# Block-sparse attention and a gated MLP on one core: a list-scheduled order, row-halved scores, a 0/1 mask product and tokens dealt two to a partition

## The chip, the cores and the metric

The kernel runs on one core of a Trainium2 chip. The metric is the time of one execution on the device in microseconds (us). The profile's span, from the first to the last instruction, is about 2 us shorter than that time. Each profile shown here is of one execution. "PE" is TensorE's matmuls, "PEld" its weight loads, "DVE" VectorE, "ACT" ScalarE, "POOL" GpSimd, "SP" the queue that issues most DMAs.

## The reference, cut to what matters

```
q, k, v: (4 batches, 8 heads, 768 tokens, 64)      block = 32 tokens
scores = q @ k.T / 8
mask   = near the diagonal | first or last block row or column | 3 sampled blocks a row
attn   = softmax(where(mask, scores, -1e9))
x      = (attn @ v) as 3072 tokens x 512
h      = x @ w_in                      # 512 -> 2048
out    = (h * sigmoid(beta * h)) @ w_out   # 2048 -> 512
```

The MLP of a group of tokens needs the attention of all eight heads for these tokens. Attention is done for a pair of heads (there are four pairs in a batch) and a stretch of queries at a time.

## The kernel before: the parts that matter

A score matmul takes one head. It contracts over 88 rows: 64 of the head and 24 more, which hold a one-hot of the key's block on one side and the mask's penalty on the other, so the masked score comes out of TensorE ready.

```python
def step(hh, kc0):                         # one head, kn chunks of 128 keys
    def run():
        sc = sc_pool.tile([P, 1024], FP32, tag="sc", name="sc")
        for i in range(kn):
            nc.tensor.matmul(sc[:, i * n:(i + 1) * n],
                lhsT=kX[0:D + NB, hh, (kc0 + i) * P:(kc0 + i + 1) * P],
                rhs=qX[0:D + NB, hh, q0:q0 + n], start=True, stop=True)
        et = et_pool.tile([P, 1024], FP16, tag="et", name="et")
        nc.scalar.activation(out=et[:, 0:kn * n], in_=sc[:, 0:kn * n],
                             func=AF.Exp, bias=0.0, scale=SCALE)
...                                        # values: 24 matmuls of 65 columns, then normalise
tiles = [(0, 0, 512), (0, 512, 256), (1, 0, 256), (1, 256, 512), ...]
n_group = N_TOK // 512                     # six MLP groups of 512 tokens
```

The order is a hand-made weave: one MLP piece after so many score steps. Keys and queries are turned on TensorE for the first five pairs, by DMA after that; the attention results are always turned on TensorE. Six consecutive tokens lie in one partition, so a load comes in pieces of 1536 bytes.

The softmax here doesn't subtract the row's maximum and nothing guards it: scores larger than these inputs give would overflow.

Of the kernel before, what the change touches and what calls it, by code (L numbers as in the profile page):

```python
# [13 lines left out]
ALU = mybir.AluOpType  # L14


@with_exitstack
def kernel(
# [17 lines left out]
    NC = S // P  # L36
    NPAIR = H // 2
# [6 lines left out]
    NEG = -30000.0  # L44

    persist = ctx.enter_context(tc.tile_pool(name="persist", bufs=1))
    stage_pool = ctx.enter_context(tc.tile_pool(name="stage", bufs=3))
    et_pool = ctx.enter_context(tc.tile_pool(name="et", bufs=13))
    work_pool = ctx.enter_context(tc.tile_pool(name="work", bufs=3))
    g_pool = ctx.enter_context(tc.tile_pool(name="g", bufs=2))  # L50




    NVA = 5
    NSTG = 2
    va_tiles = []
    for i in range(NVA):
        va_tiles.append(persist.tile([P, 2, NC, VW], FP16, name=f"va_{i}"))
    stg = {}  # L60
    for nm in ("k", "q"):
        stg[nm] = [persist.tile([P, 2, NC, P], FP16, name=f"{nm}stg_{i}") for i in range(NSTG)]

    def pair_src(x, b, j):
        return x[b, 2 * j:2 * j + 2].rearrange("h (p c) d -> p h (c d)", c=NC)

    loaded = {}

    def emit_load(b, j, eng=None):
        eng = eng or nc.sync  # L70
        sts = []
        for name, src in (("k", k), ("q", q), ("v", v)):
            st32 = stage_pool.tile([P, 2, NC * D], FP32, tag=f"{name}st", name=f"{name}st")
            if (b, j) == (1, 0) and name == "k":
                nc.gpsimd.tensor_copy(out=st32[0:1, 0, 0:1], in_=w_out_sb[0:1, 4, 0:1])
            eng.dma_start(out=st32, in_=pair_src(src, b, j))
            sts.append(st32)
        loaded[(b, j)] = sts
# [3 lines left out]

# [4 lines left out]
    beta_h_sb = persist.tile([P, N_FFC], FP32, name="beta_h_sb")  # L87

# [3 lines left out]
    def gate(w, like):  # L92
        nc.gpsimd.tensor_copy(out=w[0:1, 0, 0:1], in_=like[0:1, 0, 0:1])

    def emit_w_in(i):
        nc.gpsimd.dma_start(out=w_in_sb[:, :, i * 512:(i + 1) * 512],
                            in_=w_in_r[:, :, i * 512:(i + 1) * 512])

    def emit_w_out(i):
        nc.gpsimd.dma_start(out=w_out_sb[:, i * 4:(i + 1) * 4, :],  # L100
                            in_=w_out_r[:, i * 4:(i + 1) * 4, :])


    sc_pool = ctx.enter_context(
        tc.tile_pool(name="sc_psum", bufs=2, space=bass.MemoryType.PSUM))
    av_pool = ctx.enter_context(
        tc.tile_pool(name="av_psum", bufs=1, space=bass.MemoryType.PSUM))
    mm_pool = ctx.enter_context(
        tc.tile_pool(name="mm_psum", bufs=3, space=bass.MemoryType.PSUM))

    NSET = 5
    sets = []
    for i in range(NSET):
        sets.append((persist.tile([P, 2, S], FP16, name=f"kX_{i}"),
                     persist.tile([P, 2, S], FP16, name=f"qX_{i}")))

    onehot = persist.tile([NB, NC, P], FP16, name="onehot")
    oh_flat = onehot.rearrange("j c p -> j (c p)")
    oh_tok = persist.tile([P, NC, NB], FP16, name="oh_tok")
    mask16 = persist.tile([NB, NB], FP16, name="mask16")  # L120
    warm = persist.tile([P, 512], FP16, name="warm")
    sc_warm = []

    def emit_warm(n):
        if not sc_warm:
            sc_warm.append(sc_pool.tile([P, 1024], FP32, tag="sc", name="warm_ps"))
        for _ in range(n):
            nc.tensor.matmul(sc_warm[0][:, 0:512], lhsT=warm[:, 0:P], rhs=warm,  # L128
                             start=True, stop=True)

    def emit_first():

        sb_i32 = persist.tile([NB, 3], mybir.dt.int32, name="sb_i32")
# [3 lines left out]
        nc.sync.dma_start(out=sb_i32, in_=sb_lo)  # L137
        nc.scalar.dma_start(out=beta_sb, in_=moe_beta.rearrange("(c p) -> c p", p=P))
        for j in range(3):
            emit_load(0, j)  # L140
# [3 lines left out]
        dif = persist.tile([NB, NB], FP32, name="dif")  # L144
        nc.gpsimd.iota(dif, pattern=[[1, NB]], base=0, channel_multiplier=-1,
                       allow_small_or_imprecise_dtypes=True)
        iota_j = persist.tile([NB, NB], FP32, name="iota_j")
        nc.gpsimd.iota(iota_j, pattern=[[1, NB]], base=0, channel_multiplier=0,
                       allow_small_or_imprecise_dtypes=True)
        iota_i = persist.tile([NB, 1], FP32, name="iota_i")  # L150
        nc.gpsimd.iota(iota_i, pattern=[[0, 1]], base=0, channel_multiplier=1,
                       allow_small_or_imprecise_dtypes=True)

        nc.gpsimd.memset(oh_tok, 1.0)
        nc.gpsimd.affine_select(out=oh_tok, in_=oh_tok, pattern=[[1, NC], [-BLK, NB]],
                                compare_op=ALU.is_ge, fill=0.0, base=0,
                                channel_multiplier=NC)
        nc.gpsimd.affine_select(out=oh_tok, in_=oh_tok, pattern=[[-1, NC], [BLK, NB]],
                                compare_op=ALU.is_ge, fill=0.0, base=BLK - 1,
                                channel_multiplier=-NC)  # L160
        make_identity(nc, identity)
        for va in va_tiles:
            nc.gpsimd.memset(va[:, :, :, D:VW], 1.0)
        nc.gpsimd.tensor_copy(out=ident32, in_=identity[0:16, 0:16])
        for i in range(NSTG):
            for nm in ("k", "q"):
                nc.gpsimd.memset(stg[nm][i][:, :, :, D + NB:P], 0.0)


        emit_warm(6)  # L170
        ohp = mm_pool.tile([P, NC, P], FP16, tag="mm", name="ohp")
        for c in range(NC):
            nc.tensor.transpose(out=ohp[0:NB, c, :], in_=oh_tok[:, c, :], identity=identity)  # L173
        nc.scalar.copy(out=oh_flat, in_=ohp[0:NB].rearrange("j c p -> j (c p)"))
        emit_warm(6)

        mask_blk = persist.tile([NB, NB], FP32, name="mask_blk")
# [9 lines left out]
        sb_f32 = persist.tile([NB, 3], FP32, name="sb_f32")  # L187
        nc.vector.tensor_copy(out=sb_f32, in_=sb_i32)
        for r in range(3):
            nc.vector.scalar_tensor_tensor(out=mask_blk, in0=iota_j,  # L190
                                           scalar=sb_f32[:, r:r + 1], in1=mask_blk,
                                           op0=ALU.is_equal, op1=ALU.max)
        nc.vector.tensor_scalar(out=mask16, in0=mask_blk, scalar1=1.0,
                                scalar2=-NEG, op0=ALU.subtract, op1=ALU.mult)
        for h in range(2):
            nc.scalar.copy(out=stg["k"][0][:, h, :, D:D + NB], in_=oh_tok)
        ps = mm_pool.tile([P, NC, NB], FP32, tag="mm", name="mkt")
        for c in range(NC):
            nc.tensor.matmul(ps[:, c, :], lhsT=oh_flat[:, c * P:(c + 1) * P],
                             rhs=mask16, start=True, stop=True)  # L200
        for h in range(2):
            nc.scalar.copy(out=stg["q"][0][:, h, :, D:D + NB], in_=ps)

    def emit_more_columns():
        for i in range(1, NSTG):
            for nm in ("k", "q"):
                for h in range(2):
                    nc.scalar.copy(out=stg[nm][i][:, h, :, D:D + NB],  # L208
                                   in_=stg[nm][0][:, h, :, D:D + NB])

    def emit_beta():
        ps = mm_pool.tile([P, 512], FP32, tag="mm", name="bet")
        nc.tensor.transpose(out=ps[:, 0:N_FFC], in_=beta_sb, identity=ident32)
        nc.vector.tensor_scalar(out=beta_h_sb, in0=ps[:, 0:N_FFC], scalar1=0.5,
                                scalar2=None, op0=ALU.mult)


    prepared = {}
    n_prep = [0]

    N_PE_PREP = 5

    def emit_cast(x):
        b, j = seq[x]
        kst, qst, vst = loaded.pop((b, j))
        kX, qX = sets[x % NSET]
        va = va_tiles[x % NVA]
        for name, st32, dst in (("k", kst, kX), ("q", qst, qX)):
            st16 = stg[name][x % NSTG]
            nc.vector.tensor_copy(out=st16[:, :, :, 0:D],  # L230
                                  in_=st32.rearrange("p h (c d) -> p h c d", d=D))
            if x >= N_PE_PREP:
                nc.sync.dma_start_transpose(
                    out=dst.rearrange("p h (c s) -> p (h c) s", s=P),
                    in_=st16.rearrange("p h c e -> p (h c e)"))
        prepared[(b, j)] = (kX, qX, va, vst)

    def emit_cast_v(x):
        _, _, va, vst = prepared[seq[x]]
        nc.vector.tensor_copy(out=va[:, :, :, 0:D],  # L240
                              in_=vst.rearrange("p h (c d) -> p h c d", d=D))
# [11 lines left out]

    def attn_steps(b, j, q0, n):

        nq = n // P
        kn = 2 if n == 512 else 3
        ets = [[None] * NC, [None] * NC]

# [247 lines left out]
```

## Time and profile before

| | before |
|---|---|
| time, median | 314.4 us |
| span of the profiled run | 311.9 us |
| PE, ACT, DVE busy | 94%, 71%, 45% |

From the page of the kernel before: busy time of each engine, then the busy tenths of 40 slices of 7.8 us, the granted clock, the chain of work that ended last, and the score matmuls (count, busy us, mean ns, idle time ahead of them).

```profile
PE 291.8 (94%) x2545; PEld 163.7 (52%) x2545; DVE 139.0 (45%) x303; ACT 221.7 (71%) x292; POOL 10.7 (3%) x32
...
PE   8799889987999999999989999999999899899995
...
PEclk9999999997999999999999999999999999999999
...
PE 78%; ACT 11%; DVE 5%; DMA 3%; issue 2%; ACTq 0%
...
L265 PE MATMUL sc<-qX,kX 88*128 88x512 f16 (+1 forms) x384 | 87.4, 326 | 6.2 <-DMA qX<-qstg 3.6
```

PE busy is not a measure of work, as matmuls overlap: the mean of 326 ns is a latency. What a matmul costs TensorE is the distance from its start to the start of the next. It is read off the timeline of PE (start, length, line, operation, operands, count):

```profile
114.91 0.93 PE L292 MATMUL av<-va,et 128*128 128x65 f16 x24
115.67 0.60 PE L265 MATMUL sc<-qX,kX 88*128 88x512 f16 x2
116.11 1.03 PE L328 MATMUL hp<-xT_sb,w_in_sb 128*128 128x512 f16 x4
116.97 0.60 PE L265 MATMUL sc<-qX,kX 88*128 88x512 f16 x2
117.41 1.03 PE L328 MATMUL hp<-xT_sb,w_in_sb 128*128 128x512 f16 x4
```

24 value matmuls run from 114.91 to 115.67, 32 ns each; two scores of 512 columns from 115.67 to 116.11, 216 ns each; four hidden matmuls to 116.97, again 216 ns each. There is no gap between the kinds. In the same way a score of 256 columns is 109 ns and a transpose 56 ns.

### The profile page before, as it was taken

How to read it: one execution, taken by the hardware profiler on the slowest of the kernel's cores; microseconds unless marked ns; L12 is line 12 of the kernel's file. 1: busy time of each engine (PE TensorE's matmuls, PEld its weight loads, DVE VectorE, ACT ScalarE, POOL GpSimd, SP SyncE). 2: the span in 40 equal slices, each digit the busy share in tenths (PEclk: the TensorE clock that was granted, in tenths of full speed). 3: DMA queues.
4: the chain of work that ended last, by engine and by line, in shares of the span. 5: the costliest groups of instructions: out<-in, count | busy, mean ns of one | idle time of the engine just before them, and what ended most of it. 6: DMA issues, size and time to landing. Idle time of an engine off the chain costs nothing.

```text
span 311.9 us, 6116 instructions
## 1 busy us (share of the span) xinstructions
PE 291.8 (94%) x2545; PEld 163.7 (52%) x2545; DVE 139.0 (45%) x303; ACT 221.7 (71%) x292; POOL 10.7 (3%) x32
## 2 busy tenths in 40 slices
PE   8799889987999999999989999999999899899995
PEld 4466566653555545555545666665545455544442
DVE  7676357762134664324444256644114443235500
ACT  3998877984678879668776689889587786255511
POOL 5080000000000000000000000000000000000000
PEclk9999999997999999999999999999999999999999
DMA  6989998997065749830000099900100000010011
GB/s 177 376 167 202 204 360 288 262 258 226 34 138 185 151 141 252 190 132 34 2 0 36 34 164 280 182 2 35 36 34 34 2 2 35 36 67 0 34 69 67
DMA packets 55375, 38.41 MB, mean 123 GB/s; under 512 B 35876, under 2 KB 52276, under 8 KB 55348
## 3 DMA queue, kind: packets, MB, share of 16 engines
q1 hardware_dynamic: 51092, 33.82, 39.8%
q0 software_dynamic: 4224, 4.19, 8.3%
q8 instruction: 20, 0.33, 0.4%
q14 instruction: 7, 0.06, 0.1%
q10 hardware_dynamic: 32, 0.01, 0.0%
HBM read 27.27 MB, written 6.29 MB: 108 GB/s over the span
## 4 chain that ended last, share of the span: by engine, by line
PE 78%; ACT 11%; DVE 5%; DMA 3%; issue 2%; ACTq 0%
PE op L347 27%; PE hp L328 21%; PE sc L265 15%; PE av L292 10%; ACT et L271 6%; ACT t_sb L333 4%; DVE g L335 3%; DMA qX<-qstg 3%; PE tp L249 2%; PE warm_ps L128 1%; PE xtp L309 1%; DVE xst L298 1%; ACT qX L252 0%; DVE kstg L230 0%; PE ohp L173 0%
## 5 line engine op out<-in xcount | busy, mean ns | idle before, releaser
L271 ACT ACTIVATE et<-sc 128x1024 f16<-128x1024 f32 (+1 forms) x160 | 146.8, 939 | 43.5 <-PE sc L265 42.2
L335 DVE SCALAR_TENSOR_TENSOR g<-t_sb,hp 128x512 f16<-128x512 f16 x96 | 66.0, 688 | 99.3 <-ACT t_sb L333 98.6
L328 PE MATMUL hp<-xT_sb,w_in_sb 128*128 128x512 f16 x384 | 96.9, 380 | 3.0 <-DVE g L335 3.0
L347 PE MATMUL op<-w_out_sb,g 128*128 128x512 f16 x384 | 94.9, 381 | 0.4 <-DVE g L335 0.4
L265 PE MATMUL sc<-qX,kX 88*128 88x512 f16 (+1 forms) x384 | 87.4, 326 | 6.2 <-DMA qX<-qstg 3.6
L333 ACT ACTIVATE t_sb<-hp,beta_h_sb 128x512 f16<-128x512 f32 x96 | 66.2, 689 | 18.6 <-PE hp L328 17.3
L328 PEld LDWEIGHTS <-w_in_sb 128*128 128x128 f16 x384 | 37.3, 97 | 43.0 <-issue 4.7
L347 PEld LDWEIGHTS <-g 128*128 128x128 f16 x384 | 37.2, 98 | 42.8 <-issue 1.6
L292 PEld LDWEIGHTS <-et 128*128 128x128 f16 x1152 | 43.0, 98 | 12.1 <-ACT et L271 1.1
L265 PEld LDWEIGHTS <-kX 88*128 88x128 f16 x384 | 33.3, 98 | 25.7 <-issue 9.6
L292 PE MATMUL av<-va,et 128*128 128x65 f16 x1152 | 44.8, 193 | 1.2 <-ACT et L271 0.7
L352 ACT ACTIVATE osb<-op 128x512 f32<-128x512 f32 x24 | 14.3, 596 | 20.3 <-PE op L347 20.2
L297 DVE RECIPROCAL recip<-av 128x4 f32<-128x4 f32 x48 | 8.6, 180 | 35.1 <-PE av L292 35.0
L298 DVE TENSOR_TENSOR xst<-av,recip 128x256 f16<-128x256 f32 x48 | 20.4, 424 | 1.7
L311 DVE COPY xT_sb<-xtp 128x512 f16<-128x512 f16 (+1 forms) x32 | 11.3, 354 | 16.1 <-PE xtp L309 15.9
L309 PEld LDWEIGHTS <-xst 128*128 128x128 f16 x96 | 7.7, 97 | 10.6 <-issue 2.5
L309 PE MATMUL xtp<-identity,xst 128*128 128x128 f16 x96 | 10.8, 219 | 1.7 <-DVE g L335 1.1
L230 DVE CAST qstg<-qst 128x768 f16<-128x768 f32 x16 | 9.1, 571 | 0.5 <-DMA qst<-in_q_dram 0.5
L230 DVE CAST kstg<-kst 128x768 f16<-128x768 f32 x16 | 9.0, 562 | 0.7 <-DMA kst<-in_k_dram 0.7
L240 DVE CAST va<-vst 128x768 f16<-128x768 f32 x16 | 8.8, 552 | 0.3 <-DMA vst<-in_v_dram 0.3
L249 PE MATMUL tp<-identity,kstg 128*88 128x128 f16 x60 | 4.9, 220 | 1.9 <-DVE kstg L230 1.9
L249 PEld LDWEIGHTS <-kstg 128*88 128x88 f16 x60 | 4.1, 120 | 3.4 <-ACT qstg L208 1.4
(48 smaller groups left out, 48.3 us busy)
## 6 DMA issues: line engine op xcount, KB each, us to landing
kst<-in_k_dram SPq DMA_DIRECT2D x16, 384.0 KB, 6.0
qst<-in_q_dram SPq DMA_DIRECT2D x16, 384.0 KB, 5.9
vst<-in_v_dram SPq DMA_DIRECT2D x16, 384.0 KB, 6.0
out_dram<-osb SPq DMA_DIRECT2D x24, 256.0 KB, 2.0
w_in_sb<-in_moe_w_in_dram POOLq DMA_DIRECT2D x4, 512.0 KB, 8.2
w_out_sb<-in_moe_w_out_dram POOLq DMA_DIRECT2D x4, 512.0 KB, 16.3
kX<-kstg SPq DMA_TRANSPOSE x11, 5.2
qX<-qstg SPq DMA_TRANSPOSE x11, 4.1
```

The lines of the kernel that those rows point to most:

```text
L230: nc.vector.tensor_copy(out=st16[:, :, :, 0:D], in_=st32.rearrange("p h (c d) -> p h c d", d=D))
L249: nc.tensor.transpose(out=tp[0:D + NB, c, :], in_=st16[:, h, c, 0:D + NB], identity=identity)
L265: nc.tensor.matmul(sc[:, i * n:(i + 1) * n], lhsT=kX[0:D + NB, hh, (kc0 + i) * P:(kc0 + i + 1) * P], rhs=qX[0:D + NB, hh, q0:q0 + n], star ...
L271: nc.scalar.activation(out=et[:, 0:kn * n], in_=sc[:, 0:kn * n], func=AF.Exp, bias=0.0, scale=SCALE)
L292: nc.tensor.matmul(av[:, i, hh, :], lhsT=et[:, m * n + qc * P:m * n + (qc + 1) * P], rhs=va[:, hh, kc, 0:D + 1], start=(kc == 0), stop=(kc ...
L298: nc.vector.tensor_tensor(out=xst["t"][:, half * 2:half * 2 + 2], in0=av[:, :, :, 0:D], in1=recip.to_broadcast([P, 2, 2, D]), op=ALU.mult)
L309: nc.tensor.transpose(out=xtp[:, qc, :], in_=xstage[:, qc].rearrange("p h d -> p (h d)"), identity=identity)
L328: nc.tensor.matmul(hp[:, 0:n], lhsT=w_in_sb[:, c, f * P:(f + 1) * P], rhs=xT_sb[:, c, t0:t0 + n], start=(c == 0), stop=(c == NPAIR - 1))
L333: nc.scalar.activation(out=t_sb[:, 0:n], in_=hp[:, 0:n], func=AF.Tanh, bias=0.0, scale=beta_h_sb[:, f:f + 1])
L335: nc.vector.scalar_tensor_tensor(out=g[:, f, 0:n], in0=t_sb[:, 0:n], scalar=1.0, in1=hp[:, 0:n], op0=ALU.add, op1=ALU.mult)
L347: nc.tensor.matmul(op, lhsT=g[:, f, ts * P:(ts + 1) * P], rhs=w_out_sb[:, f, :], start=(f == 0), stop=(f == N_FFC - 1))
L352: nc.scalar.activation(out=osb, in_=op, func=AF.Copy, bias=0.0, scale=0.5)
```

## The change

It has five parts.

1. The two heads of a pair lie in the two halves of the partitions, so that their score matmuls contract over 64 rows each, in two halves of the array that can run at once.
2. The mask leaves the scores. A 0/1 mask is multiplied into the exponentials on DVE, 144 times 128x1024.
3. Two consecutive tokens lie in a partition (512-byte pieces), so that one mask tile serves pairs of chunks.
4. The MLP groups are 256, 5 x 512 and 256 tokens; attention results of batches 1 to 3, but for the very last pair, are turned by DMA; the weight loads wait until pair 3's keys are in.
5. All instructions are ordered by one list scheduler with a table of durations and tuned offsets (`BIAS`). It prices a change between 64-row and 128-row matmuls (`SWITCH`) and favours a score step behind another one.

The core of the diff, with cuts marked:

```diff
-                    nc.tensor.matmul(
-                        sc[:, i * n:(i + 1) * n],
-                        lhsT=kX[0:D + NB, hh, (kc0 + i) * P:(kc0 + i + 1) * P],
-                        rhs=qX[0:D + NB, hh, q0:q0 + n],
+                for i in range(kn):
+                    for hh in range(2):
+                        nc.tensor.matmul(
+                            at(sc)[:, hh, i * n:(i + 1) * n],
+                            lhsT=kX[hh * D:(hh + 1) * D, (kc0 + i) * P:(kc0 + i + 1) * P],
+                            rhs=qX[hh * D:(hh + 1) * D, q0:q0 + n].rearrange(
+                                "d (g c p) -> d c g p", c=CG, p=P),
...
+            def mk(eng, et=et, kc0=kc0):
+                w = n // CG
+                e = at(et).rearrange("p h (r q) -> p (h r) q", q=w)
+                m = mask01[:, kc0 // CG, q0 // CG:q0 // CG + w].unsqueeze(1).to_broadcast(
+                    [P, 2 * CG * kn, w])
+                nc.vector.tensor_tensor(out=e, in0=e, in1=m, op=ALU.mult)
...
+W_GATE = (3, "k")
...
+        if e == "PE" and n.rows != rows:
+            start, rows = start + SWITCH, n.rows
...
+    moe = [(0, Q1)] + [(t, 512) for t in range(Q1, N_TOK - Q1, 512)] + [(N_TOK - Q1, Q1)]
...
+        for n in seq:                      # the scheduler's order
+            ...n.emit(...)
```

## The prediction

> **What bounds it now.** TensorE. The page gives PE 94% of a 311.9 us span, ACT 71%, DVE 45%; the chain that ended last is 78% PE, 11% ACT. PE "busy" overlaps, so I price PE by start-to-start times in the timeline: a 512-column matmul 216 ns (the last 64 take 13.83 us), two score matmuls 0.43 us (three of 256 columns 0.32), 24 value matmuls 0.765 us, a transpose 57 ns. Multiplied by the counts: hidden and output matmuls 166 us, scores 62, values 37, transposes 12: about 277 us useful. The other 35 us are the lead before the first transposes (6.6), the end (3.5), the attention-only stretch 9-38 us, paced by back-to-back exponentials (0.91 us each), waits on transpose DMAs at 60-75 us, and small stalls.
>
> **What the change does.**
> 1. Scores contract over 64 rows, the two heads in the two halves of the array. The Trainium skill, "TensorEngine Tiling (Array Packing)", Tiling Modes, says that tiles run independently and that a change of tiling mode drains the engine. No trace here shows halves overlapping. If they do, 144 steps at about 0.22 us make 31 us instead of 62: -31.
> 2. Mode changes: the new order has 78 separate stretches of scores, so 156 changes. Before has one similar change (24-row mask matmuls to transposes), with about 100 ns between starts, where 35 were usual: estimate 0.07-0.1 us each, +11 to +16.
> 3. Transposes on PE fall from 216 to 78 (DMA does the rest): -8.
> 4. The 0/1 mask adds 144 DVE products of 128x1024 fp16. The skill, "VectorE: DVE Perf Modes", the perf-mode tier table, has tensor_tensor at 2x for 16-bit SBUF; estimate from its fixed part, 0.6-0.7 us each, so 86-100 us. A part of the casts goes to POOL and 8 of the 24 output copies to DVE. DVE becomes about 200-225 us, still below PE.
> 5. ACT: 144 exponentials at 0.91 (131) plus tanh (68), output copies 10, other copies 4: about 213, as before. Off the path except early.
> 6. First token group 256 instead of 512, so MoE matmuls begin at about 23-26 us instead of 39 and, with smaller first query loads, the first exponential at about 8 us instead of 10. Attention-only idle PE time falls by some 5-8 us.
> 7. Two tokens a partition: 512-byte pieces instead of 1536, more packets; DMA is not the bound. The padded 12x128 transposes become 6x128; 22 more carry xT, hidden if the backlog is long enough.
>
> **Sum.** PE work 166+31+37+4.5 = 239, changes 14, lead 6.5, end 3.5, idle early 5-7, stalls elsewhere 7: about 275 us of span, plus the 2.5 by which the timed median exceeds the span: **277.5 us**, range **267 to 292**. Chances: faster by over 2% 0.94, within 2% 0.04, slower 0.02.
>
> **What would show it.** Pairs of score matmuls starting a few tens of ns apart, a step (four 256s or two 512s) 0.22-0.26 us; about 0.1 us lost at each change; first hidden matmul before 28 us; PE still the chain's main part (over 65%); mask products at 0.6-0.7 us; no stretch where DVE is over 95% busy.
>
> **What would make it wrong.** Halves that don't overlap (+31); mode changes of 0.2 us (+16); mask products at 1x, 1.1 us each, making DVE the bound (about 280 us of DVE); the in-order SP queue holding loads behind a transpose that waits; DVE and POOL blocking each other; four shared accumulators ("mm") too few.

## The result, and the profile after

The changed kernel took 280.69 us (279.66 to 281.79, 4 runs), the kernel before 314.43 us beside it. The ratio is 0.894 (95% interval 0.890 to 0.898). A ratio in this text is the mean time of one kernel's fast runs over that of the other's of the same rounds, so it is not quite the ratio of the medians quoted. Executions over 1.5% slower than the fastest of the same kernel are left out of the means. All runs were fast but for three, one of groups_512 and two of keys_first, which the ratios and the times below leave out. In a second batch the changed kernel took 280.67 us, ratio 0.892.

The page of the changed kernel, the same lines and the new mask product (slices of 7 us):

```profile
PE 265.3 (95%) x2455; PEld 139.5 (50%) x2455; DVE 209.5 (75%) x424; ACT 212.9 (76%) x281; POOL 28.0 (10%) x45
...
PE   4597899999999999999999999999999999999994
...
PEclk9997799999999999999999999999999999999999
...
PE 83%; ACT 7%; DVE 4%; DMA 3%; issue 2%; SPq 0%; ACTq 0%; DVEq 0%
...
L479 DVE TENSOR_TENSOR et<-et,mask 128x1024 f16<-128x1024 f16 x144 | 98.6, 695 | 20.0 <-ACT et L470 19.7
...
L462 PE MATMUL sc<-qX,kX 64*128 64x256 f16 (+1 forms) x384 | 48.4, 342 | 4.3 <-ACT et L470 3.0
```

PE is still the bound, and from the sixth slice on it is at 9 in all but the last. Four of the first five slices are thinner. The timeline of PE in the steady part shows both halves of the score story:

```profile
149.72 2.54 PE L567 MATMUL mm<-xT_sb,w_in_sb 128*128 128x512 f16 x11
152.19 0.60 PE L462 MATMUL sc<-qX,kX 64*128 64x512 f16 x4
152.72 1.04 PE L567 MATMUL mm<-xT_sb,w_in_sb 128*128 128x512 f16 x4
153.60 1.03 PE L591 MATMUL mm<-w_out_sb,g 128*128 128x512 f16 x4
```

Four score matmuls of 512 columns take 0.53 us and not 0.86. Their single starts in the trace are 152.186, 152.189, 152.412 and 152.415: each pair starts 3 ns apart, the second pair 0.226 us after the first. The next hidden matmul starts at 152.723, 0.308 us after the last pair, where 0.216 is the pace. On the way in it is the same: 11 hidden matmuls at 0.216 are 2.376 us, and the first score comes after 2.47. Over the whole trace the step into the 64-row mode is 312 ns instead of 216 and the step out 308 (medians), so one change costs 0.094 us. There are 78 stretches of scores, so 156 changes.

The ledger of TensorE, counts times the prices above:

| us of TensorE | before | after |
|---|---|---|
| hidden and output matmuls | 165.8 | 166.0 |
| scores | 62.4 | 31.2 |
| values | 36.7 | 36.7 |
| transposes (216 and 78) | 12.1 | 4.4 |
| warm-up, mask | 3.2 | 1.0 |
| mode changes, 156 x 0.094 | 0 | 14.7 |
| sum | 280.2 | 254.0 |
| the rest of the span: not working | 31.7 | 26.1 |
| span of the profiled run | 311.9 | 280.1 |

The 31.8 us gained are thus 41 us less work, 15 us of mode changes given back, and 5.6 us less time without work. Where the remaining 26 us lie is told by the busy time of the engines in stretches of the changed kernel (stretch, length, then busy us and count of PE, PEld, DVE, ACT and POOL, granted clock, DMA share, GB/s):

```profile
0.00:18.00 18.00, 10.74 (x87) 6.26 (x88) 12.28 (x34) 8.76 (x11) 11.20 (x25) 1.00 1.01 255
18.00:43.00 25.00, 21.49 (x213) 13.74 (x213) 21.57 (x50) 23.59 (x39) 1.71 (x4) 0.86 1.04 191
43.00:230.00 187.00, 186.65 (x1849) 94.28 (x1847) 155.96 (x303) 157.99 (x195) 15.04 (x17) 1.00 0.57 134
```

I cut at the start of the 64th hidden matmul, 43.0 us here. Before it TensorE was given 22.7 us of work (changes counted), so 20.3 us are lost. From there to the start of the last matmul at 276.0 us the ledger has 230.8 us of work in 233.0 us: 2.2 us are lost. The last 4.1 us are the end. In the kernel before, the stretch from its 64th hidden matmul (74.3 us) to its last (307.9) loses 9.4 us. The stages do not match, but the new order's late stretch is nearly without waits.

### The profile page after: what moved, and what is told of

Read it like the earlier page. It is cut to its first block, busy times and chain, and to the rows that moved or that the text cites. A ratio compares the mean times of both kernels' runs of the same rounds, so it can differ in the third digit from the quotient of the medians.

```text
span 280.1 us, 6128 instructions
## 1 busy us (share of the span) xinstructions
PE 265.3 (95%) x2455; PEld 139.5 (50%) x2455; DVE 209.5 (75%) x424; ACT 212.9 (76%) x281; POOL 28.0 (10%) x45
## 4 chain that ended last, share of the span: by engine, by line
PE 83%; ACT 7%; DVE 4%; DMA 3%; issue 2%; SPq 0%; ACTq 0%; DVEq 0%
PE mm L591 29%; PE mm L567 28%; PE mm L517 12%; PE sc L462 12%; ACT et L470 5%; DMA st_k<-in_k_dram 2%; PE mm L420 1%; DMA sb_i<-in_sampled_blocks_dram 1%; DVE g L576 1%; DVE et L479 1%; ACT t_sb L572 1%; DVE s_k L395 1%; ACT qX L425 0%; DVE s_q L395 0%; ACT kX L425 0%
## 5 line engine op out<-in xcount | busy, mean ns | idle before, releaser
L470 ACT ACTIVATE et<-sc 128x1024 f16<-128x1024 f32 x144 | 142.2, 1031 | 24.7 <-PE sc L462 22.0
L479 DVE TENSOR_TENSOR et<-et,mask 128x1024 f16<-128x1024 f16 x144 | 98.6, 695 | 20.0 <-ACT et L470 19.7
L591 PE MATMUL mm<-w_out_sb,g 128*128 128x512 f16 x384 | 93.3, 380 | 0.0
L567 PE MATMUL mm<-xT_sb,w_in_sb 128*128 128x512 f16 (+1 forms) x448 | 89.9, 349 | 0.4
L576 DVE SCALAR_TENSOR_TENSOR g<-t_sb,mm 128x512 f16<-128x512 f16 (+1 forms) x112 | 66.0, 608 | 23.3 <-ACT t_sb L572 22.2
L572 ACT ACTIVATE t_sb<-mm,beta_h_sb 128x512 f16<-128x512 f32 (+1 forms) x112 | 67.8, 649 | 12.9 <-PE mm L567 12.1
L591 PEld LDWEIGHTS <-g 128*128 128x128 f16 x384 | 33.7, 98 | 43.6 <-issue 11.5
L462 PE MATMUL sc<-qX,kX 64*128 64x256 f16 (+1 forms) x384 | 48.4, 342 | 4.3 <-ACT et L470 3.0
L517 PE MATMUL mm<-va,et 128*128 128x65 f16 x1152 | 44.5, 196 | 0.0
L462 PEld LDWEIGHTS <-kX 64*128 64x128 f16 x384 | 15.5, 96 | 26.9 <-issue 21.8
L527 DVE TENSOR_TENSOR xst<-mm,recip 128x256 f16<-128x256 f32 x48 | 20.1, 419 | 0.4
```

The source lines that it names most:

```text
L462: nc.tensor.matmul(at(sc)[:, hh, i * n:(i + 1) * n], lhsT=kX[hh * D:(hh + 1) * D, (kc0 + i) * P:(kc0 + i + 1) * P], rhs=qX[hh * D:(hh + 1) ...
L470: nc.scalar.activation(out=at(et).rearrange("p h q -> p (h q)"), in_=at(sc).rearrange("p h q -> p (h q)"), func=AF.Exp, bias=0.0, scale=SCALE)
L479: nc.vector.tensor_tensor(out=e, in0=e, in1=m, op=ALU.mult)
L517: nc.tensor.matmul(a[:, i, hh, :], lhsT=at(ets[kc // kn])[:, hh, at0:at0 + P], rhs=at(va)[:, hh, kc, 0:D + 1], start=(kc == 0), stop=(kc = ...
L527: nc.vector.tensor_tensor(out=at(xs)[:, half * 2:half * 2 + 2], in0=av_ap()[:, :, :, 0:D], in1=at(rb).to_broadcast([P, 2, 2, D]), op=ALU.mult)
L567: nc.tensor.matmul(at(hb)[:, 0:n], lhsT=w_in_sb[:, c, f * P:(f + 1) * P], rhs=xT_sb[:, c, t0:t0 + n], start=(c == 0), stop=(c == NPAIR - 1))
```

## The experiments

Twelve runs were made beside the first: the changed kernel once more, and eleven altered kernels. Besides the total, two times are read from each trace: the "early" time up to the start of the 64th hidden matmul, and the "late" time from there to the start of the last matmul. The instruction order is the changed kernel's own where the last column says so. Where it is not, a longer time also holds what the new order costs, as the offsets were tuned for the old one.

| run | time | early | late | same order |
|---|---|---|---|---|
| changed kernel | 280.69 | 43.0 | 233.0 | yes |
| after_again | 280.67 | 41.8 | 233.2 | yes |
| same_half | 315.99 | 52.6 | 257.8 | yes |
| full_rows | 293.26 | 42.6 | 245.0 | yes |
| mask_tiny | 280.63 | 41.0 | 233.2 | yes |
| warm12_repeat3 | 284.63 | 46.4 | 233.4 | yes |
| big_pieces | 280.63 | 42.0 | 233.0 | yes |
| mask_twice | 346.01 | 55.1 | 286.4 | yes |
| gate_early | 295.57 | 53.5 | 235.9 | no |
| keys_first | 281.93 | 41.2 | 234.8 | no |
| bias_zero | 289.06 | 47.6 | 236.6 | no |
| groups_512 | 295.65 | (73.4) | (216.3) | no |
| before_halves | 316.98 | | | before's |

### after_again: the yardstick

No edit. 

> The changed kernel unchanged, as the yardstick of this batch: ratio to before 0.894, within 0.004.

Measured: 280.67 us, ratio 0.892 (0.891 to 0.893). The early time of one kernel moves by about a microsecond from trace to trace, the late time by 0.2.

### same_half: no overlap of the halves

```diff
-                            lhsT=kX[hh * D:(hh + 1) * D, (kc0 + i) * P:(kc0 + i + 1) * P],
-                            rhs=qX[hh * D:(hh + 1) * D, q0:q0 + n].rearrange(
+                            lhsT=kX[0:D, (kc0 + i) * P:(kc0 + i + 1) * P],
+                            rhs=qX[0:D, q0:q0 + n].rearrange(
```

> The changed kernel with both heads' score matmuls in the same half of the array (rows 0 to 63); wrong result on purpose, instruction order unchanged. Theory (TensorE is the bound and the two halves overlap, second start 3-6 ns after the first): each of 192 pairs then takes twice as long, 192 x 0.216/2 + 192 x 0.109/2 = 31 us more, so about 311 us, 1.11 of the changed kernel, and mode changes stay at about 0.094 us. Rival (scores are hidden behind exponentials or mask products, the gain came from the order): under 8 us more.

Measured: 315.99 us (313.89 to 316.24), ratio to before 1.005. Its timeline:

```profile
171.14 1.89 PE L567 MATMUL mm<-xT_sb,w_in_sb 128*128 128x512 f16 x8
172.96 1.03 PE L462 MATMUL sc<-qX,kX 64*128 64x512 f16 x4
173.93 2.76 PE L567 MATMUL mm<-xT_sb,w_in_sb 128*128 128x512 f16 x12
```

Four scores now take 0.97 us, 0.44 more than with both halves. The late stretch has 144 scores of 256 and 164 of 512 columns; unpaired they should cost 144 x 0.0545 + 164 x 0.108 = 25.6 us more, and the late time grew by 24.8. The early time grew by 10 us beside that, which I had not expected: TensorE ran at half its pace until 44.2 us, where the trace's first clock record lies. The overlap is shown. This run as a whole is no faster than the kernel before, but 10 us of that are its slow early stretch: the next run, also without overlap, shows what the other parts of the change are worth.

The two heads' scores were wrong on purpose here and in the next run, but the outputs still passed the comparison.

### full_rows: no overlap and no change of mode

```diff
-                            lhsT=kX[hh * D:(hh + 1) * D, (kc0 + i) * P:(kc0 + i + 1) * P],
-                            rhs=qX[hh * D:(hh + 1) * D, q0:q0 + n].rearrange(
+                            lhsT=kX[0:P, (kc0 + i) * P:(kc0 + i + 1) * P],
+                            rhs=qX[0:P, q0:q0 + n].rearrange(
```

> The changed kernel with the score matmuls over all 128 rows (both heads summed, wrong on purpose), order unchanged: no overlap, and no change of tiling mode. Theory (156 mode changes cost 0.094 us each on the critical path): 31 us more for the lost overlap, 14.6 less for the changes, so 16 us more than the changed kernel, about 297 us, and 14.6 us below same_half. Rival (the changes only shift idle time): the same time as same_half within 3 us.

Measured: 293.26 us (293.03 to 293.35), 12.6 us above the changed kernel and 20.7 below the kernel before (ratio 0.934). So in this order the halves bring 12.6 us after their changes of mode are paid, and the other parts of the change together bring the larger share.

```profile
161.38 1.89 PE L567 MATMUL mm<-xT_sb,w_in_sb 128*128 128x512 f16 x8
163.11 1.03 PE L462 MATMUL sc<-qX,kX 128*128 128x512 f16 x4
163.97 2.75 PE L567 MATMUL mm<-xT_sb,w_in_sb 128*128 128x512 f16 x12
```

Eight hidden matmuls are followed by the score after 1.73 us and not 1.82 as in same_half, and the four scores take 0.86, not 0.97. In the late stretch there are 124 changes, 11.7 us by the price of 0.094; same_half's late time is 12.8 us above this one. So the changes are paid in full: they do not hide in idle time. The total of same_half is 22.7 above, more than the 14.6 expected; the other 10 us are same_half's early stretch, 52.6 us against 42.6. The early score work is the same in both; the 32 changes of mode there are 3 us by the price, and the clock was full from 17.2 us here and from 44.2 us there. The other 7 us are thus put down to the clock, which no run varied alone.

### before_halves: the halves alone, in the old order

```diff
+                at = (0, 512, 256)
                 for i in range(kn):
+                    r = slice(D * (i % 2), D * (i % 2) + D)
                     nc.tensor.matmul(
-                        sc[:, i * n:(i + 1) * n],
-                        lhsT=kX[0:D + NB, hh, (kc0 + i) * P:(kc0 + i + 1) * P],
-                        rhs=qX[0:D + NB, hh, q0:q0 + n],
+                        sc[:, at[i]:at[i] + n],
+                        lhsT=kX[r, hh, (kc0 + i) * P:(kc0 + i + 1) * P],
+                        rhs=qX[r, hh, q0:q0 + n],
```

(The transposes that fill kX and qX were widened to 128 rows, so that all rows are defined.)

> The kernel before with only its score matmuls halved: 64 rows, alternating halves inside a step, everything else and the order unchanged (no mask in the scores, so the masking is wrong on purpose). Theory: pairs save 96 x 0.216 + 64 x 0.109 = 28 us, but the old order has 142 separate score stretches, 284 mode changes at 0.094 us = 27 us, so nothing is left: 314 us, within 4 us. Rival (halving alone pays, the order is beside the point): 285 to 292 us.

Measured: 316.98 us, ratio to before 1.009 (1.005 to 1.013).

```profile
116.27 0.39 PE L267 MATMUL sc<-qX,kX 64*128 64x512 f16 x2
116.59 1.04 PE L330 MATMUL hp<-xT_sb,w_in_sb 128*128 128x512 f16 x4
117.56 0.39 PE L267 MATMUL sc<-qX,kX 64*128 64x512 f16 x2
117.88 1.04 PE L330 MATMUL hp<-xT_sb,w_in_sb 128*128 128x512 f16 x4
```

A pair of scores is down from 0.44 to 0.32 us, which includes the change out of the 64-row mode, and the four hidden matmuls behind it take 0.97 instead of 0.86, as the change into the next scores is paid there. From one score stretch to the next it is 1.29 us, where before had 1.30. The halving on its own brings nothing in an order with 142 score stretches. In the new order, which has 78, it pays (full_rows).

### bias_zero: the list scheduler without its tuned offsets

```diff
-BIAS = {"av": 39, "beta": 625, ... "x turn": -13}
+BIAS = dict.fromkeys(("av", "beta", ... "x turn"), 0)
```

> The changed kernel with all the tuned offsets of the list scheduler at zero: plain earliest start. 103 score stretches instead of 78, so 50 more mode changes at 0.094 us = 5 us more. Theory: 284 to 290 us, 5 us of it changes of mode, the rest waits. Rival (any list order does as well): within 2 us of the changed kernel.

Measured: 289.06 us (288.52 to 290.25), as the theory had it. It has 206 changes instead of 156, 4.7 us; the rest of the 8.4 us are waits (in its late stretch 5.9 us are lost, not 2.2). An untuned list order with the other parts of the change still gets three quarters of the gain.

### mask_tiny and mask_twice: is VectorE in the way?

```diff
 mask_tiny
-                nc.vector.tensor_tensor(out=e, in0=e, in1=m, op=ALU.mult)
+                nc.vector.tensor_tensor(out=e[:, :, 0:1], in0=e[:, :, 0:1], in1=m[:, :, 0:1],
+                                        op=ALU.mult)
 mask_twice
                 nc.vector.tensor_tensor(out=e, in0=e, in1=m, op=ALU.mult)
+                nc.vector.tensor_tensor(out=e, in0=e, in1=m, op=ALU.mult)
```

> The mask product on one column of each group instead of all (wrong result on purpose), same number and order of instructions: VectorE loses about 80 of its 209 busy us. Theory (PE bound; VectorE holds things up only in the first 40 us, where PE loses about 20 us): 2 to 5 us less than the changed kernel, almost all of it before 45 us. Rival (VectorE's latency between exponential and values is on the chain throughout): 10 us less or more.

Measured: 280.63 us, the time of the changed kernel. Stretches of mask_tiny, cut at the same places of its order:

```profile
18.00:41.00 23.00, 19.48 (x205) 12.41 (x202) 12.06 (x47) 22.46 (x36) 0.96 (x4) 0.93 1.13 209
41.00:228.00 187.00, 186.52 (x1848) 94.14 (x1847) 100.46 (x304) 158.08 (x194) 14.09 (x17) 1.00 0.58 133
```

DVE falls from 156 to 100 us in the late stretch (third busy figure) and the stretch stays at 187 us. The early time is 0.8 to 2 us shorter in the trace, but the timed runs show nothing. Both theories expected a gain; both fall. Over the whole span DVE lost 67 us of its 209.5 and nothing was gained. The instructions themselves stayed, at 179 ns each on average instead of 695, so what is shown to be free is their length, not the extra step between exponential and values.

> The mask product done twice (0/1, so the result stays right): VectorE gets 144 x about 0.62-0.69 us = 90 to 99 us more and becomes the bound at about 300 us busy. Theory: 310 to 325 us. If VectorE had room to spare the time would stay below 290.

Measured: 346.01 us, still right, and more than I expected. DVE is busy 301 us, and over 97% of the stretch from 40 to 260 us (107.58 and 107.81 of 110):

```profile
40.00:150.00 110.00, 89.98 (x833) 47.06 (x834) 107.58 (x206) 74.17 (x96) 6.28 (x7) 0.92 0.40 97
150.00:260.00 110.00, 92.24 (x774) 43.49 (x773) 107.81 (x189) 75.34 (x93) 11.50 (x12) 0.97 0.52 121
260.00:345.00 85.00, 78.78 (x628) 41.73 (x625) 53.64 (x102) 44.96 (x66) 0.00 (x0) 0.98 0.12 41
```

My estimate forgot that the MLP left over at the end has no mask products, so the last 85 us leave DVE a third idle. TensorE was also at half its clock for several stretches here, the longest from 29.3 to 46.3 us. What the run shows is the margin: with one product DVE has room, with two it is the bound.

### warm12_repeat3: the clock in the first 32 us

The trace's clock records of the changed kernel start at 18.2 us with the full clock, fall to half at 25.0 and are full again from 31.8. The page's row of tenths shows 9 before 18 us too, but there is no record there, and the timeline contradicts it (start, length, ..., count):

```profile
15.51 0.83 PE L420 MATMUL mm<-identity,s_k 128*128 128x128 f16 x6
16.13 0.42 PE L420 MATMUL mm<-identity,s_q 128*128 128x128 f16 x2
...
18.54 0.51 PE L420 MATMUL mm<-identity,s_k 128*128 128x128 f16 x6
18.96 0.29 PE L420 MATMUL mm<-identity,s_q 128*128 128x128 f16 x2
...
25.80 0.61 PE L462 MATMUL sc<-qX,kX 64*128 64x512 f16 x2 [0.38 <-ACT et L470]
26.34 1.50 PE L517 MATMUL mm<-va,et 128*128 128x65 f16 x24
27.77 0.61 PE L462 MATMUL sc<-qX,kX 64*128 64x512 f16 x2
```

Six transposes take 0.62 us at 15.5 and 0.42 at 18.5 (medians 106 and 56 ns each), and 24 values take 1.43 us at 26.3 instead of 0.77. The experiment keeps TensorE busier with work that changes no result:

```diff
-        emit_warm(4)
+        emit_warm(12)
...
-                for i in range(kn):
+                early = x < NPAIR and (q0 == 0 or x < 2)
+                for i in list(range(kn)) * (3 if early else 1):
```

> 12 warm-up matmuls instead of 4, and every score matmul of the first 24 steps issued three times (same result), so that TensorE is not granted half its clock before 18 us and between 25 and 32 us. Theory A (the half clock of the first 32 us costs time: values products there took 1.45 us instead of 0.77): the clock is full from about 6 us on and 2 to 4 us less. Theory B (the early pace is set by loads, casts and exponentials, since full_rows, whose clock stayed full from 17 us on, began its hidden matmuls at 33.3 us as against 33.6): the clock is full, the first hidden matmul stays at 32 to 34 us, the time within 1 us.

Measured: 284.63 us (283.49 to 285.94), 4 us worse. The clock was full from 6.8 us on but for 13.6 to 17.0, and values from 21.8 us on took the full pace:

```profile
21.76 0.94 PE L518 MATMUL mm<-va,et 128*128 128x65 f16 x24
22.63 1.48 PE L463 MATMUL sc<-qX,kX 64*128 64x256 f16 x24
...
29.03 0.93 PE L518 MATMUL mm<-va,et 128*128 128x65 f16 x24
```

But the first hidden matmul came at 36.3 us instead of 33.6: the 12th exponential started at 26.3 us and not at 23.8, as the extra scores come before the exponentials in TensorE's order. Theory A is not borne out by this run, and theory B, which expected no change of time, missed too. A warm clock alone, without the filler's cost, was not tried, so the run does not clear the half clock. Traces with the same order point to a cost: in after_again the half clock lasted 3.4 us (from 26.0) and not 6.8, and the hidden matmuls began 1.2 us sooner; in same_half it lasted to 44.2 us, and the early stretch took 10 us more than in full_rows.

### big_pieces: 1536-byte loads

```diff
-            hg = src[b, 2 * j:2 * j + 2].rearrange("h (g p c) d -> p (h g) (c d)", g=NG, p=P)
...
+            big = src[b, 2 * j:2 * j + 2].rearrange("h (p c) d -> p h (c d)", c=NC)
+            nc.sync.dma_start(out=at(st)[:, :, lo * D:hi * D], in_=big[:, :, lo * D:hi * D])
```

> Six tokens a partition in the loads alone, as before the change: pieces of 1536 bytes (512 and 1024 for the split queries) instead of 512; the order is unchanged, tokens are permuted so masks do not fit (wrong on purpose). 512-byte pieces took 32 ns each and 1536-byte ones 72 ns, so batch 0's 4.7 MB cost 17.7 us of all engines instead of 14. Theory (loads pace the first 20 us): the 12th exponential starts 1.5 to 3 us earlier than 23.8, the first hidden matmul too, and 1 to 3 us less in total. Rival (loads are hidden): under 0.5 us.

Measured: 280.63 us, no gain. Its output is wrong, which doesn't matter for the time. At 16 us 96% of batch 0's bytes were in, as against 83 and 86% in the two traces of the changed kernel, and the 12th exponential started at 23.5 us instead of 23.4 to 23.8. The smaller pieces cost DMA time that nothing waits for.

### gate_early: weights sooner

```diff
-W_GATE = (3, "k")
+W_GATE = (1, "k")
```

> The changed kernel with the weight loads gated on the keys of pair 1 instead of pair 3. Theory (the first hidden matmul at 33.6 us waits for the attention of four pairs, not for the weights, which landed at 25 us): weights land some 3 to 5 us earlier, the first hidden matmul stays within 2 us of 33.6 and the time within 2 us, perhaps 1 to 2 worse since the other loads share the wire. Rival (late weights cost the 8 us by which I misjudged the start of the hidden matmuls): first hidden matmul at or before 29 us and 3 to 5 us less.

Measured: 295.57 us, 15 us worse. My theory had said 2, the rival a gain; both fall.

```profile
16.50 1.03 PE L462 MATMUL sc<-qX,kX 64*128 64x256 f16 x8
23.07 0.39 PE L420 MATMUL mm<-identity,s_q 128*128 128x128 f16 x2 [5.54 <-POOL s_q L395]
```

From 17 to 23 us TensorE has nothing to do: it waits for a cast of pair 3's queries on POOL, and that cast waited 11.3 us for its load, which shares the wire with the weights. The clock stays low until 42.2 us, and the early time is 53.5 us. With the gate two pairs earlier the kernel is thus 15 us slower. The order was made anew and the clock was low throughout the early stretch, so the wait shown is a part of the 15 us that these runs do not separate from the rest.

### keys_first: values behind the next pair's keys

The values of each pair of batch 0 are loaded and cast after the next pair's keys and queries (a reordering of the calls that make the nodes).

> The changed kernel with each pair's values loaded behind the next pair's keys and queries; scheduled anew, right result. If loads pace the first 20 us, the 12th exponential starts 1 to 2.5 us earlier and the time falls by 1 to 2 us; a new order may also lose some us, as the offsets were tuned for the old one, so only a fall tells something.

Measured: 281.93 us (the four fast runs, 280.92 to 284.4; two slow ones took 285.48 and 286.4). The 12th exponential started at 21.8 us, 2 us earlier, and the early time fell to 41.2; the late stretch lost 4.5 us instead of 2.2. As announced, a rise tells nothing, since the offsets were tuned to another order. Inconclusive.

### groups_512: six equal MLP groups

```diff
-    moe = [(0, Q1)] + [(t, 512) for t in range(Q1, N_TOK - Q1, 512)] + [(N_TOK - Q1, Q1)]
+    moe = [(t, 512) for t in range(0, N_TOK, 512)]
```

> The changed kernel with six groups of 512 tokens instead of 256, 5 x 512, 256; scheduled anew. Theory: the first hidden matmul has to wait for 36 exponentials instead of 12, so until about 48 to 52 us TensorE has only attention work (about half of its time); 6 to 12 us more than the changed kernel. Rival (the early stretch is paid back later, since exponentials are then ahead): within 2 us.

Measured: 295.65 us (the three fast runs, 292.66 to 296.61; a slow one took 297.36), 15 us worse, more than the 6 to 12 expected. The first hidden matmul comes at 56.2 us, after 36 exponentials, and the clock fell to half three times on the way (34.4, 44.7 and 51.5 us). In its timeline values wait for the mask products, then the hidden matmuls start at half the pace, four in 1.85 us:

```profile
52.70 2.54 PE L517 MATMUL mm<-va,et 128*128 128x65 f16 x43 [0.83 <-DVE et L479]
...
56.17 1.91 PE L567 MATMUL mm<-xT_sb,w_in_sb 128*128 128x512 f16 x4
58.02 0.74 PE L462 MATMUL sc<-qX,kX 64*128 64x512 f16 x4
```

Without the small first group the kernel is 15 us slower, of which the low clock and the untuned order are parts that are not separated. None of the altered kernels beat the changed kernel by more than the noise (the best two took 280.63 us).

## Why the prediction was right, point by point

- **TensorE is the bound, before and after: right.** The chain is 83% PE. With the changed order, late work plus changes accounts for the late time within 2.2 us of 233, and adding score work moves it nearly one for one (same_half: 24.8 of 25.6 us).
- **Scores 62 to 31 us: right.** Pairs start 3 ns apart; a step of four 256s or two 512s is 0.22 to 0.24 us without its changes. The Trainium skill, "TensorEngine Tiling (Array Packing)", Tiling Modes, says that tiles run in parallel, and "TensorE: Matmul & The Clock Gate", Part 3, has about 4 ns between their starts; this trace agrees, and same_half shows the worth, 24.8 us in the late stretch alone.
- **156 mode changes at 0.07 to 0.1 us, 14 us in the sum: right.** Measured 0.094 us each, 14.7 us. "TensorEngine Tiling (Array Packing)", Tiling Modes, also says that a mode change drains the engine; the 0.094 us lost at each change agree with that. (The clue in the trace of before was one such change with 98 ns between starts, where the mask matmuls ahead of it start 25 ns apart.) before_halves shows that this term decides whether the halving pays at all.
- **Transposes -8: right.** 12.1 to 4.4 us.
- **Mask products at 0.6 to 0.7 us, DVE 200 to 225 us, not the bound: right.** The estimate leans on the skill's "VectorE: DVE Perf Modes", the perf-mode tier table, which has tensor_tensor at 2x for 16-bit data in SBUF; the trace agrees, with a mean length of 0.695 us for 1024 columns and 0.60 us between the starts of two products in a row. DVE is busy 209.5 us, and mask_tiny shows no gain from taking 67 us of it away. One sign failed: DVE was to be over 95% busy nowhere, but it is busy throughout from 45 to 55 us (mask_tiny, with 81% in its busiest 10 us, shows that this cost nothing measurable).
- **ACT about 213 us: right,** 212.9.
- **DMA is not the bound: right for the piece size** (big_pieces). It was too bold for the early loads: in gate_early TensorE waits 5.5 us for a load, and the run is 15 us slower.
- **"MoE matmuls begin at about 23-26 us", "idle early 5-7" on top of a lead of 6.5: wrong.** They began at 33.6 us (32.4 in the second trace), and 20.3 us of TensorE were lost before 43 us (19.1), where the two terms gave 11.5 to 13.5. Nor did the idle time in the stretch with attention alone fall by 5 to 8 us: ahead of its first hidden matmul the kernel before lost 11.1 us by these prices, the changed one 19.5 (18.4 in the second trace), as each exponential there still takes 0.9 us but comes with half the score work, and the clock is half for a part of it. I had counted 12 exponentials ahead of the first hidden matmul; in the order that was made, 20 have started by then. The first half of the weights landed 10.0 us after an issue at 15.2, so at 25.2, and was not what it waited for.
- **"stalls elsewhere 7": too large.** The late stretch lost 2.2 us. The end was 4.1 instead of 3.5.

So the total was right within 3.2 us because two terms were off in opposite directions, +8 early and -5 late. That these nearly cancel was luck, though either error alone would have left the time within the range.

What stays open is what exactly holds the first 40 us. The length of the mask products and the size of the load pieces were each tried alone and found not to matter there. The half clock was not tried alone, and the traces named under warm12_repeat3 say that it costs something. A late 12th exponential is not enough of a reason: in bias_zero and keys_first, each in its own order, it started at 20.7 and 21.8 us, and the hidden matmuls still began at 32.4 and 31.9, with 19 and 21 exponentials started. ACT is busy 23.59 of the 25 us from 18 to 43, so exponentials look like the pace of that stretch, and the order puts the values of pairs 2 and 3 (26.3 and 30.2 us) behind scores that wait for ACT. That is argued from the trace; no run put the values first.

## What to carry to other kernels

Price matmuls by start-to-start times, count them, and set the sum against the span: what is left says whether to remove work or waits. Two heads in two halves of the array halve the score time, but every switch between 64-row and full-row matmuls cost 0.094 us here, so the gain is set by how many stretches the order has, and should be computed before the layout is rewritten. Work added on an engine with room can be free (cutting the mask products from 98.6 to 24.7 us gained nothing measurable), while the first microseconds are sensitive: the two runs that changed who loads first, and how soon the bound engine gets its main work, were each 15 us slower, the low clock that followed included.

## What the Trainium skill lacked or had wrong

- "TensorEngine Tiling (Array Packing)", Tiling Modes, says that a mode switch drains the engine but has no figure. Here a switch between 64-row and 128-row matmuls in a full stream cost 0.092 to 0.096 us each way (308 and 312 ns between starts instead of 216).
- "TensorE: Matmul & The Clock Gate", Part 1, the table of the two states, has the half clock after at least one idle window. Here the clock fell to half at 25.0 us after a 3.4 us window in which TensorE issued 21 matmuls, some 40% of what the full pace allows by the prices above, and in groups_512 after windows of 40%, 30% and 23%; windows of 50% and more kept it. In between, 39% (keys_first) and 44% (bias_zero) kept it and 42% (big_pieces) did not, so the limit is not sharp in these traces.
- "DMA: Bandwidth & Descriptors", Specifications, gives 512 bytes as the least transfer for full rate. Here packets of 512 bytes took 31 ns on average, 16 GB/s an engine, and packets of 1536 bytes 73 ns, 21 GB/s.
- "TensorE: Matmul & The Clock Gate", Part 1, calls the clock events of a trace unreliable at times, but no page says that the record can begin late. The changed kernel's first record is at 18.2 us; before it the profile's row reads full, while transposes start 106 ns apart instead of 56.
